# The reverse scan of a preparation queued behind the decays' scan of the one before

## The chip, the cores and the metric

The kernel runs on one core of a Trainium2 chip. The core has a matrix engine (TensorE, PE in the profile), a vector engine (VectorE, DVE), a scalar engine (ScalarE, ACT), GpSimd (POOL) and SyncE (SP), which here only starts transfers; 16 DMA engines move data between HBM and the on-chip memory. Each engine works through its own queue of instructions in the order in which they were put there, and waits at an instruction until what it needs is there. The metric is device time in microseconds for the whole program.

## The reference

Two parts follow each other: a linear-attention recurrence over 768 steps for 4 batches of 8 heads with head dimension 40, and a soft mixture of 8 expert networks over the 3072 resulting tokens.

```python
for t in range(S):                       # state: (B, H, 40, 40), S = 768
    y[:, :, t] = einsum('bhd,bhde->bhe', r[t], state)
    Sa = einsum('bhde,bhe->bhd', state, a[t])
    state = state * w[t][:, :, None, :] - einsum('bhd,bhe->bhde', Sa, b[t])
    state = state + einsum('bhd,bhe->bhde', v[t], k[t])
x = y.transpose(0, 2, 1, 3).reshape(3072, 320)
P = exp(x @ w_gate - max)                # 8 rounds of row and column normalisation follow
out = sum over e of P[:, e] * (relu(x @ w1[e]) @ w2[e])    # 320 -> 1024 -> 320
```

All is float32. The decay `w` lies near 0.9 for every step and every column of the state.

## The kernel before

**Attention in chunks.** The 768 steps are cut into 12 chunks of 64, so that a chunk of one batch becomes a few small matrix products. A *preparation* `prep(c, b)` does what depends only on the inputs of chunk c and batch b; there are 48, numbered `cb = 4c + b` from 0. It loads one input block (`inp`, L120: decays, k, b and a), and then:

- the *reverse scan* `q` (L126, VectorE): running products of the decays from the end of the chunk backwards, 112 rows of 260. There is one buffer `q` for all preparations;
- the reciprocal `g1` of the whole chunk's decay (L130, VectorE; one buffer);
- the *decays' scan* `ge` (L135, VectorE): running products from the front, started with `g1`. It is written into the preparation's *set* (tiles `sx`, `bb`, `cc`, `ge`; some sets lie in one raw tile named `st` in the profile). There are 19 sets used in turn (`NSX`), so preparation n writes where n-19 was;
- `kb` = k and b times q (L146) and `cc`, a copy out of q (L151), both on GpSimd (the first `kb` on VectorE); `ab` = a times the decays (L152, L153, on GpSimd from the seventh preparation on), four small matmuls `ll` (L158) and four transposes `kt` (L166) on TensorE, the masked copy `sx` (L168, VectorE), copies on ScalarE (L154, L155, L172 to L175), and the part `lt` sent to HBM (`ld`, L177).

The input block of most preparations has two buffers; the load of the one after next waits for the `ab` product that reads a buffer last.

**The inversion.** Two chunks (8 preparations) form a group. Their triangular matrices are read back from HBM (`load_lu`, L370) and inverted on VectorE: `flip_l` (two copies, L199 and L200, the inversion's first), multiply and reduce pairs (L183/L186, L192/L195) into `un` and `tn`, with a last copy at L360. There are six groups and so six inversions. The inverses go to HBM and come back (`tload`, L239 to L246), and TensorE completes them (`gp` L255, `op` L261) to the matrix `tt` of a chunk.

**The recurrence.** `recur(c, b)` has per chunk and batch: loads `rv` (L269) and `f` (L271), matmuls `av` (L280) and a masked copy `f` (L281, VectorE), `xc` (L288) and copies `x` and `c` (L294, L295), `pu` (L299) with the masked copy `pm` (L301, VectorE), `c2` (named `c`, L306) with the sum `ws` (L308, VectorE), the output `y` = ws times the set's decays (L312, GpSimd; it is the last reader of the set's `ge`), and the next state `z` (L321) with its transposes (L326).

**Expert layers.** From about 460 us on TensorE runs them nearly without a break (L571 first layer, L636 second).

**What sets the order.** The program text lists the pieces of preparation, inversion and recurrence in the order of due times:

```python
t = max(t, t0 + P0[s] + PD * i) if s else -20 + 0.01 * i
ev.append((t, do_prep, (s,) + cb + (i == 0,)))
...
for _, fn, args in sorted(ev, key=lambda x: x[0]):
    fn(*args)
```

That order is only a priority. A planner of the framework then walks through the program on a simulated clock, and whenever an engine comes free it gives it, of the instructions that are ready by that clock, the one that is earliest in the text. The result is fixed at build time as one queue for each engine. From the ninth block of the expert layers on (`N_MAN`) the order of the text is kept on all engines but SyncE. `tc.issue_after(ins)` adds to each instruction in its block that goes to the engine of `ins` an ordering edge behind `ins`, without a semaphore.

Of the kernel before, what the change touches and what calls it, by code (L numbers as in the profile page):

```python
# [3 lines left out]

# [10 lines left out]
ALU = mybir.AluOpType  # L15
# [14 lines left out]
def attention(ctx, tc, d, xd, ps, pq, pt, gs, lg):  # L30
    nc = tc.nc
# [13 lines left out]
    one65 = cst[0:RL, 400:660]  # L45
# [55 lines left out]
    def first_use(i):  # L101
        if i in fresh:
            fresh.discard(i)
            nc.gpsimd.memset(bb_b[i], 0.0)
            nc.scalar.copy(out=sx_b[i][64:R2].rearrange("r p h x -> r (p h) x")[:, :, 64:104],
                           in_=cst[64:R2, 360:400].unsqueeze(1).broadcast_to([40, 8, 40]))
# [3 lines left out]
    def rot(key, lst):  # L110
        i = state[key]
        state[key] = (i + 1) % len(lst)
        return lst[i]

    zp = [None] * NB

    def prep(c, b, ld):
        cb = c * NB + b
        inp = raws[IN_MAP[cb]][0:RL, 0:1032] if IN_MAP.get(cb) else pin.tile([RL, 1032], F32, name="inp", bufs=2)
        nc.sync.dma_start(out=inp, in_=d["inp"][c, b, :, 0:1032])  # L120
        w65 = inp[:, 0:264]
        kb_in = inp[0:R2, 264:776].rearrange("r (p k t) -> r p k t", p=NP, k=2)
        a_in = inp[:, 776:1032].rearrange("r (p t) -> r p t", p=NP)
        qr = pin.tile([RL, NP, 65], F32, name="q")
        q = qr[:, ::-1]
        nc.vector.tensor_tensor_scan(  # L126
            out=qr.rearrange("r p t -> r (p t)"), data0=w65[:, 260:0:-1], data1=one65,
            initial=0.0, op0=ALU.mult, op1=ALU.add)
        g1 = rot("g1", g1_b)
        nc.vector.reciprocal(out=g1[:, :, 0], in_=q[:, :, 64])  # L130
        sx = rot("sx", sx_b)
        i = next(j for j in range(NSX) if sx_b[j] is sx)
        bb, cc, ge = bb_b[i], cc_b[i], ge_b[i]
        g = ge[:, :, 0:64]
        nc.vector.tensor_tensor_scan(  # L135
            out=ge.rearrange("r p t -> r (p t)"), data0=w65[:, 0:260],
            data1=g1.rearrange("r p t -> r (p t)"), initial=0.0, op0=ALU.mult, op1=ALU.add)
        if cb < NKB:
            raw = raws[KB_SETS[cb % len(KB_SETS)]]
            kb = raw[0:R2, 0:512].rearrange("r (p k t) -> r p k t", p=NP, k=2)  # L140
            lt = raw[0:64, 512:1024].rearrange("r (p k t) -> r p k t", p=NP, k=2)
        else:
            kb = pin.tile([R2, NP, 2, 64], F32, name="kb")
            lt = pin.tile([64, NP, 2, 64], F32, name="lt")
        eng = nc.vector if cb < NFAST else nc.gpsimd
        (nc.gpsimd if cb in KB_POOL else eng).tensor_tensor(  # L146
            out=kb, in0=kb_in,
            in1=q[0:R2, :, 63::-1].unsqueeze(2).broadcast_to([R2, NP, 2, 64]), op=ALU.mult)
        ab = rot("ab", ab_b)
        first_use(i)  # L150
        nc.gpsimd.tensor_copy(out=cc, in_=q[0:R2, :, 64])  # L151
        eng.tensor_tensor(out=ab[0:40, :, 0:64], in0=a_in[0:40], in1=g[0:40], op=ALU.mult)  # L152
        eng.tensor_tensor(out=ab[64:104, :, 64:128], in0=a_in[64:104], in1=g[64:104], op=ALU.mult)  # L153
        nc.scalar.copy(out=sx[64:104, :, 0, 0:64], in_=ab[0:40, :, 0:64])  # L154
        nc.scalar.copy(out=sx[64:104, :, 1, 0:64], in_=ab[64:104, :, 64:128])  # L155
        ll = pq.tile([128, NP, 2, 64], F32, name="ll", tag="pq")
        for p in range(NP):
            nc.tensor.matmul(ll[:, p], lhsT=kb[:, p], rhs=ab[:, p], start=True, stop=True)  # L158
        if cb < NKB:
            nc.scalar.activation(out=lt, in_=ll[64:128], func=AF.Copy, scale=-1.0)  # L160
            (nc.sync if cb < N_SP else nc.scalar).dma_start(out=ld[GRP[c][1], :, b], in_=lt)
            kt = pt.tile([128, NP, 2, 64], F32, name="kt", tag="pt")
        else:
            kt = pq.tile([128, NP, 2, 64], F32, name="kt", tag="pq")
        for p in range(NP):
            nc.tensor.transpose(kt[:, p].rearrange("s h x -> s (h x)")[:, 0:R2],  # L166
                                kb[:, p].rearrange("r k s -> r (k s)"), ident[0:R2, 0:R2])
        nc.vector.tensor_tensor(  # L168
            out=sx[0:64, :, :, 0:64], in0=ll[0:64],
            in1=mask_u.unsqueeze(1).unsqueeze(1).broadcast_to([64, NP, 2, 64]), op=ALU.mult)  # L170
        if cb >= NKB:
            nc.scalar.activation(out=lt, in_=ll[64:128], func=AF.Copy, scale=-1.0)  # L172
        nc.scalar.copy(out=sx[0:64, :, :, 64:104], in_=kt[0:64, :, :, 0:40])
        nc.scalar.activation(out=bb[0:64, :, 0:40], in_=kt[64:128, :, 0, 0:40], func=AF.Copy, scale=-1.0)
        nc.scalar.activation(out=bb[64:128, :, 64:104], in_=kt[64:128, :, 1, 0:40], func=AF.Copy, scale=-1.0)  # L175
        if cb >= NKB:
            (nc.sync if cb < N_SP else nc.scalar).dma_start(out=ld[GRP[c][1], :, b], in_=lt)  # L177
        return dict(cc=cc, g=g, sx=sx, bb=bb)
# [201 lines left out]
    def do_prep(s, c, b, first):  # L380
        if first:
            start_seg(s)
        preps[c, b] = prep(c, b, invs[s][0])

    for c in range(NCH):
# [3 lines left out]
        t = 5 * c + 2 - T_LEAD  # L389
        ev.append((t - L_LEAD, tload, (c,)))  # L390
        ev.append((t, tmat, (c,)))
    for s, cs in enumerate(GROUPS):
# [3 lines left out]
        for i in range(n):  # L396
            cb = (cs[0] + i // NB, i % NB)
            j = cb[0] * NB + cb[1] - NSX
            t = 5 * (j // 4) + 3 + SKEW * (j % 4) + 0.01
            t = max(t, t0 + P0[s] + PD * i) if s else -20 + 0.01 * i  # L400
# [27 lines left out]
N_SP = 8  # L428
# [25 lines left out]
def body(ctx, tc, d, out):  # L454
# [9 lines left out]
    with ExitStack() as actx:  # L464
        ps, pq, pt = (actx.enter_context(tc.tile_pool(name=f"a_ps{i}", bufs=n, space=bass.MemoryType.PSUM))
                      for i, n in enumerate((PC, PQ, PT)))
        nc.sync.dma_start(out=gs, in_=d["gate"])
        attention(actx, tc, d, xd, ps, pq, pt, gs, lg)
# [356 lines left out]
```

## Time and profile before

| what | value |
|---|---|
| median of 3 runs (lowest to highest) | 1821.08 us (1817.26 to 1829.43) |
| the profiled execution's own time | 1816.42 us |
| its span | 1814.0 us |
| busy PE, DVE, ACT, POOL | 1686.0, 1366.1, 842.8, 876.6 us |
| q scans (L126) from tile `inp`: count, busy, idle of VectorE before them | 42, 34.1 us, 36.4 us |

A row of the groups gives line, engine, operation, output and inputs by their names, shapes and count; then busy time and the mean of one in ns; then the idle time of the engine just ahead of them and what ended it. A row of the timeline gives start and duration in us, the engine, the line and the instruction, and in brackets how long the engine stood idle before it and what ended that. The slices of the page give busy tenths of forty equal parts of the span.

### The profile page before, as it was taken

The page shows a single profiled execution, that of the slowest core. Times are in us where ns is not written, and L with a number is a line of the kernel's source. Part 1 is how long each engine was busy: PE and PEld are TensorE (multiplying, and loading weights), DVE is VectorE, ACT ScalarE, POOL GpSimd, SP SyncE. Part 2 cuts the span into 40 slices and gives each one's busy share as a digit, 9 for nine tenths or more (in the row PEclk, how much of TensorE's full clock was granted, in tenths as well). Part 3 has the DMA queues.
Part 4 walks back from the last instruction along what each step waited for, and adds up shares of the span by engine and source line. Part 5 has one row for each costly group of instructions (what it writes and reads, how often), then busy time and mean ns, then how long its engine had stood idle before and what let it go on. Part 6 is the DMA issues. An engine that isn't in the chain of part 4 may idle for free.

```text
span 1814.0 us, 32745 instructions
## 1 busy us (share of the span) xinstructions
PE 1686.0 (93%) x12611; PEld 1662.1 (92%) x12611; DVE 1366.1 (75%) x2353; ACT 842.8 (46%) x1811; POOL 876.6 (48%) x850
## 2 busy tenths in 40 slices
PE   5478888987889999999999999999999999999999
PEld 4367888887889999999999999999999999999999
DVE  7886976974788777767686778867686777768675
ACT  6357767765634443424343443435343443434342
POOL 7555645724453554728173554009173553719160
PEclk7569989998989999999999999999999999999999
DMA  7478678668221111102010112202010111102001
GB/s 200 106 160 197 150 173 192 153 142 200 75 67 36 41 38 38 58 20 76 8 69 20 57 38 72 58 1 76 14 63 22 55 38 38 58 20 76 18 21 44
DMA packets 178736, 135.61 MB, mean 75 GB/s; under 512 B 119189, under 2 KB 160789, under 8 KB 178581
## 3 DMA queue, kind: packets, MB, share of 16 engines
q1 hardware_dynamic: 174901, 127.79, 26.8%
q10 hardware_dynamic: 3680, 5.74, 1.2%
q8 instruction: 99, 1.62, 0.4%
q14 instruction: 56, 0.46, 0.1%
HBM read 111.48 MB, written 22.02 MB: 74 GB/s over the span
## 4 chain that ended last, share of the span: by engine, by line
PE 72%; DVE 6%; DMA 2%; issue 1%; SPq 1%; ACT 1%; POOL 1%; DVEq 0%; ACTq 0%; POOLq 0%
PE op L636 37%; PE p L571 34%; DVE pr L192 1%; DVE sm L589 1%; DVE hl L595 1%; DVE gt L195 0%; DMA ld<-lt 0%; PE xc L288 0%; DMA rv<-in_rv_dram 0%; DVE un L195 0%; PE pu L299 0%; DVE u L589 0%; DMA ws<-in_wts_dram 0%; DVE xch L559 0%; DMA lu<-ld 0%
## 5 line engine op out<-in xcount | busy, mean ns | idle before, releaser
L571 PE MATMUL p<-xch,wh 128*128 128x384 f32 (+1 forms) x1792 | 605.7, 339 | 10.2 <-DVE u L589 4.3
L592 ACT ACTIVATE hh<-sm 128x384 fp32r<-128x384 f32 x512 | 269.4, 527 | 723.0 <-DVE sm L589 722.9
L636 PE MATMUL op<-wh,hh 128*128 128x320 f32 x1536 | 477.1, 311 | 1.1 <-ACT hh L592 0.9
L636 PE MATMUL op<-wl,hh 128*128 128x320 f32 x1536 | 474.8, 310 | 0.0
L636 PE MATMUL op<-wh,hl 128*128 128x320 f32 x1536 | 468.2, 310 | 0.9 <-DVE hl L595 0.9
L517 POOL TENSOR_TENSOR wl<-ws,wh 128x640 fp32r<-128x640 f32 x60 | 103.6, 1726 | 606.3 <-ACT wh L515 606.1
L595 DVE SCALAR_TENSOR_TENSOR hl<-sm,hh 128x384 fp32r<-128x384 f32 x512 | 375.0, 766 | 1.8 <-ACT hh L592 1.3
L571 PEld LDWEIGHTS p<-xch,wh 128*128 128x128 f32 (+1 forms) x1792 | 337.2, 188 | 14.3 <-DVE u L589 6.0
L571 PE MATMUL p<-xcl,wh 128*128 128x384 f32 x896 | 302.6, 338 | 0.0
L571 PE MATMUL p<-xch,wl 128*128 128x384 f32 x896 | 301.7, 337 | 0.0
L636 PEld LDWEIGHTS op<-wh,hh 128*128 128x128 f32 x1536 | 290.3, 189 | 2.2 <-ACT hh L592 1.9
L636 PEld LDWEIGHTS op<-wl,hh 128*128 128x128 f32 x1536 | 291.1, 190 | 0.0
L636 PEld LDWEIGHTS op<-wh,hl 128*128 128x128 f32 x1536 | 287.3, 188 | 1.3 <-DVE hl L595 1.2
L589 DVE TENSOR_TENSOR sm<-p,u 128x384 f32<-128x384 f32 x384 | 236.1, 625 | 8.8
L571 PEld LDWEIGHTS p<-xcl,wh 128*128 128x128 f32 x896 | 168.7, 188 | 0.0
L571 PEld LDWEIGHTS p<-xch,wl 128*128 128x128 f32 x896 | 168.6, 188 | 0.0
L589 DVE TENSOR_TENSOR sm<-p,p 128x384 f32<-128x384 f32 x128 | 71.3, 557 | 128.7 <-PE p L571 74.7
L589 DVE TENSOR_TENSOR p<-p,p 128x384 f32<-128x384 f32 x128 | 71.2, 556 | 99.6 <-PE p L571 99.1
L589 DVE TENSOR_TENSOR u<-p,p 128x384 f32<-128x384 f32 x128 | 70.8, 554 | 57.6 <-PE p L571 56.4
L158 PE MATMUL ll<-ab,kb 104*128 104x128 f32 x336 | 62.4, 343 | 51.8 <-POOL ab L153 32.3
L158 PEld LDWEIGHTS ll<-ab,kb 104*128 104x128 f32 x336 | 53.4, 241 | 58.3 <-POOL ab L153 35.8
L525 POOL TENSOR_TENSOR wl<-ss,wh 128x512 fp32r<-128x512 f32 x60 | 90.1, 1502 | 27.6 <-ACT wh L522 23.4
(164 smaller groups left out, 2637.0 us busy)
## 6 DMA issues: line engine op xcount, KB each, us to landing
ws<-in_wts_dram SPq DMA_DIRECT2D x60, 832.0 KB, 4.4
inp<-in_inp_dram SPq DMA_DIRECT2D x42, 451.5 KB, 4.8
rv<-in_rv_dram SPq DMA_DIRECT2D x48, 336.0 KB, 4.1
xd<-y SPq DMA_DIRECT2D x24, 224.0 KB, 3.1
ld<-lt ACTq DMA_DIRECT2D x40, 128.0 KB, 2.9
f<-in_vt_dram SPq DMA_DIRECT2D x48, 80.0 KB, 3.1
out_dram<-acc SPq DMA_DIRECT2D x42, 80.0 KB, 2.1
lu<-ld SPq DMA_DIRECT2D x24, 128.0 KB, 3.2
```

The lines of the kernel that those rows point to most:

```text
L158: nc.tensor.matmul(ll[:, p], lhsT=kb[:, p], rhs=ab[:, p], start=True, stop=True)
L192: nc.vector.tensor_tensor(out=prv, in0=a.unsqueeze(2).broadcast_to([nu, n_c, n_r, n_k]), in1=m.unsqueeze(1).broadcast_to([nu, n_c, n_r, n_ ...
L517: g.tensor_tensor(out=wl[:, 0:640], in0=raw[:, 256:896], in1=wh[:, 0:640], op=ALU.subtract)
L525: g.tensor_tensor(out=lv[:, 3:7], in0=so[:, :, 0], in1=hv[:, 3:7, 0], op=ALU.subtract)
L571: nc.tensor.matmul(o, lhsT=w_, rhs=x_, start=(j == 0), stop=(j == 3))
L589: eng.tensor_tensor(out=out, in0=x, in1=y, op=ALU.add)
L592: nc.scalar.activation(out=hh[:, f, h], in_=sm[f][:, h], func=AF.Relu)
L595: v.scalar_tensor_tensor(out=hl[:, f, h], in0=sm[f][:, h], scalar=0.0, in1=hh[:, f, h], op0=ALU.max, op1=ALU.subtract)
L636: nc.tensor.matmul(ops[i], lhsT=a[:, h, cs], rhs=w_[:, cw], start=(f == 0 and h == 0 and j == 0), stop=(last and h == 1 and j == 2))
```

## The change

The scan `ge` of every preparation is noted in a list as it is written. From preparation 8 on (`N_SP` is 8, so the ninth) the reverse scan `q` is written inside a block that orders it on VectorE behind the last noted `ge`, which is that of the preparation before. The first eight preparations are untouched. No operation, buffer or transfer is added or taken away.

```diff
+    scans = []
 
     def prep(c, b, ld):
...
         qr = pin.tile([RL, NP, 65], F32, name="q")
         q = qr[:, ::-1]
-        nc.vector.tensor_tensor_scan(
-            out=qr.rearrange("r p t -> r (p t)"), data0=w65[:, 260:0:-1], data1=one65,
-            initial=0.0, op0=ALU.mult, op1=ALU.add)
+        with tc.issue_after(scans[-1].ins) if cb >= N_SP else nullcontext():
+            nc.vector.tensor_tensor_scan(
+                out=qr.rearrange("r p t -> r (p t)"), data0=w65[:, 260:0:-1], data1=one65,
+                initial=0.0, op0=ALU.mult, op1=ALU.add)
         g1 = rot("g1", g1_b)
         nc.vector.reciprocal(out=g1[:, :, 0], in_=q[:, :, 64])
...
-        nc.vector.tensor_tensor_scan(
+        scans.append(nc.vector.tensor_tensor_scan(
             out=ge.rearrange("r p t -> r (p t)"), data0=w65[:, 0:260],
-            data1=g1.rearrange("r p t -> r (p t)"), initial=0.0, op0=ALU.mult, op1=ALU.add)
+            data1=g1.rearrange("r p t -> r (p t)"), initial=0.0, op0=ALU.mult, op1=ALU.add))
```

More of the change, by code (lines that the diff above doesn't have):

```diff
@@ L1 @@
 from collections import deque
-from contextlib import ExitStack
+from contextlib import ExitStack, nullcontext
 from functools import partial
```

## The prediction

> **What bounds the kernel now.** I began with the page: the span, then the busy tenths.
>
> ```profile
> span 1814.0 us, 32745 instructions
> ...
> PE   5478888987889999999999999999999999999999
> ...
> DVE  7886976974788777767686778867686777768675
> ...
> DMA  7478678668221111102010112202010111102001
> ```
>
> The profiled execution took 1816.42 us, 2.42 more than its span, and lies 4.66 under the median of 1821.08. From the thirteenth slice on (each is 45.35 us) PE stands at 9 throughout and DMA at 2 and below: the expert layers run on TensorE, their first matmuls at 459 us. The preparations lie ahead of that, their last scan at 359:
>
> ```profile
> 459.11 0.60 PE L571 MATMUL p<-xch,wh 128*128 128x384 f32 x2
> ```
> ```profile
> L135 DVE TENSOR_TENSOR_SCAN st<-inp,g x17: 681/700/1674, 46.6 to 359.0; 112x260 f32<-112x260 f32 x17
> ```
>
> So the change can move the time only by letting the attention part end sooner or later. The windows show what is full there.
>
> ```profile
> 272.00:317.00 45.00, 37.41 (x444) 35.97 (x445) 28.68 (x54) 32.19 (x81) 25.29 (x33) 0.93 0.89 193
> 317.00:363.00 46.00, 41.63 (x494) 40.15 (x493) 45.55 (x79) 35.97 (x91) 34.53 (x35) 0.96 0.63 154
> ```
>
> The columns are the stretch, its length, busy PE, PEld, DVE, ACT and POOL, granted clock, DMA share, GB/s. In the first stretch the DMA engines are 89% busy and VectorE 64%; in the second VectorE is busy 45.55 of 46 us. VectorE is an in-order queue here, and the groups by form say what it stands for in front of a q scan:
>
> ```profile
> L126 DVE TENSOR_TENSOR_SCAN q<-inp,cst 112x260 f32<-112x260 f32 x42 | 34.1, 811 | 36.4 <-DMA inp<-in_inp_dram 30.3 <-POOL kb L146 6.0
> ```
>
> 30.3 us it waited for the load of a preparation's input, with everything queued behind the scan waiting too.
>
> **What the change touches.** I matched the n-th q scan with the n-th decays' scan (48 each) in VectorE's timeline. Counting preparations from 0, q(n+1) stands ahead of the decays' scan ge(n) at ten places, n = 19, 22, 25, 26, 27, 35, 37, 41, 43, 44; from preparation 8 on it stands behind it everywhere else already. So 30 of the 40 new orderings hold in the queue of before, and ten pairs swap. Nothing is added or removed: no scan, no DMA. Both ends of the new edge are on VectorE, where order needs no wait. No instruction moves past another queue by the edge itself.
>
> Why q overtook: there are 19 sets, so ge(n) writes into the set whose decays the y product of preparation n-19 (GpSimd) reads last. ge(n) is ready at the end of that y; q(n+1) needs only its input and the free q buffer. The first of the ten and the last:
>
> ```profile
> 123.35 2.18 POOL L312 TENSOR_TENSOR y<-ws,ge 104x256 f32<-104x256 f32 x1
> ```
> ```profile
> 126.02 0.88 DVE L135 TENSOR_TENSOR_SCAN ge<-inp,g 112x260 f32<-112x260 f32 x1
> ```
> ```profile
> 337.00 0.69 POOL L312 TENSOR_TENSOR y<-ws,ge 104x256 f32<-104x256 f32 x1
> ```
> ```profile
> 339.24 0.67 DVE L135 TENSOR_TENSOR_SCAN ge<-inp,g 112x260 f32<-112x260 f32 x1
> ```
>
> The scans come 0.49 and 1.55 us after their y ended (125.53, 337.69). Over the ten places this lateness sums to 17.9 us, the largest 5.11 (n=41) and 3.20 (n=25): that is all that the swap itself can give. I go through the places with the rest of each queue held as it is.
>
> **n=41.**
>
> ```profile
> 307.40 0.57 DVE L308 TENSOR_TENSOR ws<-c,c 104x416 f32<-104x416 f32 x1
> 312.74 0.70 DVE L126 TENSOR_TENSOR_SCAN q<-inp,cst 112x260 f32<-112x260 f32 x1 [4.77 <-DMA inp<-in_inp_dram]
> 313.36 0.56 DVE L301 TENSOR_TENSOR pm<-pu,cst 128x416 f32<-128x416 f32 x1
> 313.84 0.69 DVE L135 TENSOR_TENSOR_SCAN ge<-inp,g 112x260 f32<-112x260 f32 x1
> ...
> 315.74 0.49 DVE L199 COPY lu<-lu 128x128 f32<-128x128 f32 x1 [0.94 <-DMA lu<-ld]
> ```
> ```profile
> 307.00 1.06 PE L299 MATMUL pu<-x,tt 128*128 128x104 f32 x8
> ```
> ```profile
> 308.05 0.68 POOL L312 TENSOR_TENSOR y<-ws,ge 104x256 f32<-104x256 f32 x1 [0.42 <-DVE ws L308]
> ```
>
> q(42) waits 4.77 us for its input, and behind it stand the recurrence's pm (its pu was there at 308.06) and ge(41) (its y ended at 308.73). Swapped, pm runs at 308.1, ge(41) at 308.7, q(42) still at 312.74. That looks like 5 us, but the next thing in the queue is the first copy of the fifth inversion, which waits for its matrix until 315.74 either way, and the recurrence's next f and ws stand behind that copy. I take it at 0. If the planner also put that f ahead of the copy, the full stretch after it would be shorter by it, and with pm and ge (0.56, 0.69) that is some 1.9 us:
>
> ```profile
> L281 DVE TENSOR_TENSOR f<-av,cst 104x512 f32<-104x512 f32 x48 | 32.5, 678 | 14.6 <-PE av L280 13.8 <-DMA nd<-tn 0.5
> ```
>
> **n=25.**
>
> ```profile
> 171.07 0.70 DVE L126 TENSOR_TENSOR_SCAN q<-inp,cst 112x260 f32<-112x260 f32 x1 [2.84 <-DMA inp<-in_inp_dram]
> 171.69 0.67 DVE L135 TENSOR_TENSOR_SCAN ge<-inp,g 112x260 f32<-112x260 f32 x1
> ...
> 175.69 0.27 DVE L199 COPY lu<-lu 128x128 f32<-128x128 f32 x1 [2.47 <-DMA lu<-ld]
> ```
> ```profile
> 167.81 0.68 POOL L312 TENSOR_TENSOR y<-ws,ge 104x256 f32<-104x256 f32 x1
> ```
> ```profile
> 173.98 2.08 PE L158 MATMUL ll<-ab,kb 104*128 104x128 f32 x8 [3.67 <-POOL ab L153]
> ```
>
> ge(25) was ready at 168.49 and VectorE was free; it ran at 171.69, and PE stood 3.67 us at the preparation's matmuls. Swapped, those come 3.2 us sooner; but here too the next copy of an inversion waits for its load until 175.69, and what the recurrence has next on VectorE is queued behind it. Taken at 0; 3.2 if that cover is gone.
>
> **n=26 and n=37**, where the DMA wait of q is short and VectorE has other work:
>
> ```profile
> 179.55 0.56 DVE L183 TENSOR_TENSOR pr<-un,lu 128x64 f32<-128x64 f32 x1
> 180.61 0.70 DVE L126 TENSOR_TENSOR_SCAN q<-inp,cst 112x260 f32<-112x260 f32 x1 [0.50 <-DMA inp<-in_inp_dram]
> 181.23 0.68 DVE L135 TENSOR_TENSOR_SCAN ge<-inp,g 112x260 f32<-112x260 f32 x1
> ```
> ```profile
> 277.91 0.67 DVE L168 TENSOR_TENSOR sx<-ll,cst 64x512 f32<-64x512 f32 x1
> 279.39 0.83 DVE L126 TENSOR_TENSOR_SCAN q<-inp,cst 112x260 f32<-112x260 f32 x1 [0.81 <-DMA inp<-in_inp_dram]
> 280.14 1.19 DVE L195 TENSOR_REDUCE un<-pr 128x64 f32<-128x1024 f32 x1
> 281.25 0.68 DVE L135 TENSOR_TENSOR_SCAN ge<-inp,g 112x260 f32<-112x260 f32 x1
> ```
> ```profile
> 278.99 0.67 POOL L312 TENSOR_TENSOR y<-ws,ge 104x256 f32<-104x256 f32 x1
> ```
>
> n=26: ge at 180.11, q at 180.79, both done at 181.49 in place of 181.91: 0.42. n=37: the reduce at 278.58, ge at 279.77 (its y ended at 279.66), q at 280.45, done at 281.28 in place of 281.93: 0.65. Both lie in queues that are nearly full, so I count them on the path. The other six (n = 19, 22, 27, 35, 43, 44) trade one scan for the other in a queue that goes on at once or meets the same y: 0 each, bounded by their lateness of 6.3 together above, and below by one scan of 0.7 at each for q(n+1), which its readers on GpSimd would feel, 4.2 together. That cover is the y of the next preparation: the scan after next cannot start before it, some 7 us later.
>
> Sum: 0.42 + 0.65 = 1.1 us sooner; 1815.3 for the profiled execution, 1820.0 from the median.
>
> One thing speaks against it: with ge(n) first, the ab products that wait for ge on GpSimd run while q(n+1) is on VectorE. Such a pair stands in the trace already:
>
> ```profile
> 321.81 1.19 DVE L126 TENSOR_TENSOR_SCAN q<-inp,cst 112x260 f32<-112x260 f32 x1
> ```
> ```profile
> 321.58 0.86 POOL L152 TENSOR_TENSOR ab<-inp,ge 40x256 f32<-40x256 f32 x1
> ```
>
> q took 1.19 there in place of 0.70. At ten places that is 4.9 us at most; I take 0, since at six of the ten q waits for its load anyway (below). The Trainium skill, page "SBUF — State Buffer", section "Who interferes with whom", has the rule: a VectorE instruction with two SBUF inputs and a GpSimd one that reads SBUF shut each other out for a whole instruction. The 1.19 agrees; by the rule the sum would be 4.9 - 1.1 = 3.8 us slower, 1825.
>
> **Rivals.** (a) All the lateness is on the path: ge(n) sets ab, ll and the buffer of the next input. For it: PE's 3.67 us above. Against: the two copies that wait for their loads anyway. 17.9 us give 1803; with the six waits of q for its input at the swapped places gone as well (1.55 and 0.39 below, 2.84, 0.50, 0.81 and 4.77 above, 10.9 in all), 1792.
>
> ```profile
> 147.67 0.70 DVE L126 TENSOR_TENSOR_SCAN q<-inp,cst 112x260 f32<-112x260 f32 x1 [1.55 <-DMA inp<-in_inp_dram]
> ...
> 189.14 0.92 DVE L126 TENSOR_TENSOR_SCAN q<-inp,cst 112x260 f32<-112x260 f32 x1 [0.39 <-DMA inp<-in_inp_dram]
> ```
>
> (b) Loads set the pace: where DMA is 89% busy an earlier ge only brings an earlier request into a full queue. Then nothing moves: 1821.
>
> (c) Slower. The planner lays out every queue anew, SyncE's too. The input's load waits there for the ab that frees its buffer:
>
> ```profile
> SPq L120 <- POOL ab L153: 13.1, 9, 2.7
> ```
>
> That is between 100 and 320 us: 13.1 us in 9 waits, the longest 2.7. If the new plan, which thinks ge(n) earlier, puts that load ahead of the recurrence's rv and f loads, SyncE stands at it, and these land late. Ten such places at 2.7 are 27: 1821 - 1 + 27 = 1847. It decides against the change by over 1% from the eighth of them on ((18.2 + 1.1) / 2.7).
>
> (d) It does not do what it says: the planner keeps the ten q scans where they were in time and holds ge too, or the swap is undone by other work put between. 1821.
>
> **How the numbers follow.** Forecast 0.45, a 0.18, b 0.15, c 0.15, d 0.07. The time is the forecast's, 1820. Its own range is 1815 (1.9 and 3.2 from the covers gone) to 1825 (4.2 from q's readers and half a microsecond over). About what a measurement of this kernel can tell from no change is 1%, 18 us: under 1803, over 1839. Faster takes most of (a), 0.14; slower most of (c), 0.12; 0.74 are left for the middle. The range reaches half-way into (a) and (c): 1802 to 1837.
>
> **What would show it.** VectorE's timeline has ge(n) ahead of q(n+1) at all ten places, and its lateness after the y falls to some 0.7 us; the 30.3 us that q waits for its input stay within a few us; the inversions' first copies start at the same times to 2 us; the first expert matmul (459 us) moves by no more than 3. A first expert matmul that moves by over 10 us would prove the forecast wrong, and the inversion whose first copy moved first would say by which rival.

## The result, and the profile after

Over 14 runs each the median went from 1821.68 to 1812.07 us: 9.6 us between the medians. The ratio of the runs, by which all kernels are compared here, is 0.9942 with a 95% interval from 0.9925 to 0.9959. That is 10.6 us faster (7.5 to 13.7). The forecast was 1820.0 in a range from 1802 to 1837; it said that the time would stay within 1%, which it does, but it gave the change 1.1 us.

The profiled execution of the changed kernel took 1813.25 us, that of before 1816.42. The latter was a quick draw, 5.3 us under its median, so the two traces show less of a difference than the runs. In the changed kernel the lines of a preparation ahead of the scan q have moved down by one, those from the scan on by two. The page after:

```profile
span 1811.3 us, 32736 instructions
...
PE   5468978898889999999999999999999999999999
...
DVE  6887986974788677768686778867686777767675
...
DMA  8478688577311111102010112202010111102001
```

It is the same picture: TensorE at 9 from the thirteenth slice on. The difference lies ahead of that. The recurrence's last y on GpSimd, in the timeline of before and then of the changed kernel (start, duration, in brackets the idle time before it and what ended it):

```profile
488.22 1.40 POOL L312 TENSOR_TENSOR y<-ws,st 104x256 f32<-104x256 f32 x1 [2.77 <-DVE ws L308]
```
```profile
483.31 0.94 POOL L314 TENSOR_TENSOR y<-ws,st 104x256 f32<-104x256 f32 x1 [4.41 <-DVE ws L310]
```

The attention part ends 5.4 us sooner (489.62 and 484.25). From there to the end of the profiled execution it is 1326.8 us before and 1329.0 after, 2 us more; the last section has what ends in these 2 us. The first expert matmul, in the timeline of the changed kernel, has moved the other way, from 459.11 to 460.71:

```profile
460.71 0.60 PE L573 MATMUL p<-xch,wh 128*128 128x384 f32 x2
```

The two windows of the prediction, of the changed kernel (stretch, length, busy PE, PEld, DVE, ACT, POOL, granted clock, DMA share, GB/s):

```profile
272.00:317.00 45.00, 38.18 (x460) 36.74 (x459) 29.48 (x55) 32.66 (x83) 26.82 (x33) 0.92 0.89 199
317.00:363.00 46.00, 40.63 (x479) 39.11 (x479) 42.78 (x73) 34.32 (x86) 29.75 (x34) 0.93 0.56 139
```

DMA is as full in the first as it was (0.89). VectorE is busy for 42.78 us of the second, where it was 45.55. The place n=41 in VectorE's timeline, and the group of the q scans:

```profile
303.12 0.93 DVE L137 TENSOR_TENSOR_SCAN ge<-inp,g 112x260 f32<-112x260 f32 x1 [0.20 <-POOL y L314]
...
307.24 0.70 DVE L128 TENSOR_TENSOR_SCAN q<-inp,cst 112x260 f32<-112x260 f32 x1 [3.19 <-DMA inp<-in_inp_dram]
307.86 0.56 DVE L303 TENSOR_TENSOR pm<-pu,cst 128x416 f32<-128x416 f32 x1
...
312.96 0.29 DVE L201 COPY lu<-lu 128x128 f32<-128x128 f32 x1 [3.87 <-DMA lu<-ld]
```
```profile
L128 DVE TENSOR_TENSOR_SCAN q<-inp,cst 112x260 f32<-112x260 f32 x42 | 33.1, 789 | 23.8 <-DMA inp<-in_inp_dram 19.0 <-POOL kb L148 4.7
```

ge(41) now runs the moment its y ends (0.03 us behind it, 5.11 before), ahead of q(42). Over the ten places the lateness is 7.9 us, 0.79 each; it was 17.9. The loads that q waits for cost VectorE 19.0 us of idle time instead of 30.3.

The planner, though, did more than swap ten pairs. Compared position by position, 341 of VectorE's 2353 queue places hold another instruction than before, 984 of TensorE's 10586, 355 of ScalarE's, 92 of GpSimd's and 144 of SyncE's.

### The profile page after: what moved, and what is told of

It is laid out like the page before. It is cut to its first block, busy times and chain, and to the rows that moved or that the text cites. A ratio compares the mean times of both kernels' runs of the same rounds, so it can differ in the third digit from the quotient of the medians.

```text
span 1811.3 us, 32736 instructions
## 1 busy us (share of the span) xinstructions
PE 1691.7 (93%) x12611; PEld 1668.9 (92%) x12611; DVE 1361.3 (75%) x2353; ACT 842.0 (46%) x1811; POOL 868.8 (48%) x850
## 4 chain that ended last, share of the span: by engine, by line
PE 75%; DVE 11%; DMA 5%; issue 3%; POOL 2%; SPq 2%; ACT 2%; ACTq 0%; DVEq 0%; POOLq 0%
PE op L638 36%; PE p L573 34%; DVE pr L194 1%; PE xc L290 1%; DVE q L128 1%; DMA lu<-ld 1%; PE pu L301 1%; SPq L248 1%; DMA inp<-in_inp_dram 1%; DVE un L197 1%; DMA rv<-in_rv_dram 1%; DVE sm L591 1%; DVE gt L197 1%; POOL ab L154 1%; DMA ld<-lt 1%
## 5 line engine op out<-in xcount | busy, mean ns | idle before, releaser
L597 DVE SCALAR_TENSOR_TENSOR hl<-sm,hh 128x384 fp32r<-128x384 f32 x512 | 368.5, 753 | 1.9 <-ACT hh L594 1.3
```

What stands on the lines that cost most here:

```text
L597: v.scalar_tensor_tensor(out=hl[:, f, h], in0=sm[f][:, h], scalar=0.0, in1=hh[:, f, h], op0=ALU.max, op1=ALU.subtract)
```

## The experiments

Two theories stood against each other. By the first, the swap of the ten pairs is the cause: ge is no longer held up, and what comes sooner reaches the end. By the second, the new edge only nudges the planner into another layout of all the queues, and the time lies there. Times below are ratios to the kernel before, run beside it, with 95% intervals; microseconds are the ratio on 1821.

**The swap alone, twice.** All five queues of before are written out by hand in the program, as a chain of ordering edges that lets the planner choose nothing. Only the ten q scans move. In the diff, n stands for 19, 22, 25, 26, 27, 35, 37, 41, 43, 44.

```diff
+def queue_up(nc, tc):
+    for numbers in QUEUES.values():       # those of the kernel before
+        for x, y in zip(numbers, numbers[1:]):
+            tc.add_manual_dep(by[f"I-{y}"], f"I-{x}", info, reason="queue_up")
...
 # VectorE's queue, at ten n
-    q(n+1)
     ...
     ge(n)
+    q(n+1)
```

> Every engine's queue of the kernel before is written out by hand, and on VectorE alone the ten q scans are put right behind the decays' scan that they overtook; nothing else moves. Theory A (the gain comes from the planner's new layout of all queues, not from the swap): the last y product in the profile comes 0 to 2 us sooner than before's 489.6, and the time is 0 to 3 us under before's. Theory B (the swap itself gives it, by the lateness of the decays' scans): the last y near 483, the time 7 to 11 us under before's.

> All ten pairs swapped in the queues of before, again, against the same runs of before as the two runs above. The first time it was 7.7 us under before's (4.9 to 10.4). If the swap is about three quarters of the change's gain: 6 to 9 us under before. If that first value was high by chance: 3 to 5.

Measured: 0.9958 (0.9943 to 0.9973), and in the repetition 0.9974 (0.9959 to 0.9989). Together 0.9966, some 6.2 us. The first value is the one that the lateness theory named, and the repetition's 4.7 us lie where its expectation put them if the first was high by chance. So the swap does reach the end without any help of the planner, with more than five times the 1.1 us that the forecast gave it. The q scans' group in the first of the two:

```profile
L128 DVE TENSOR_TENSOR_SCAN q<-inp,cst 112x260 f32<-112x260 f32 x42 | 33.4, 794 | 28.2 <-DMA inp<-in_inp_dram 22.8 <-POOL kb L148 5.3
```

With nothing but the swap, the load waits fall from 30.3 to 22.8 us. Of this fall 6.7 us lie at the six swapped places where q had waited for its load: ge now runs inside the wait, at n=41 pm too, and less of it is left. The scans q themselves came hardly sooner: q(23), q(26) and q(42) started 1.01, 2.57 and 4.01 us behind the end of the y of their place before, and 0.89, 2.29 and 3.58 us with the swap.

**The changed kernel again**, for the planner's share.

> The changed kernel again, on the same chip and against the same runs of before as the three kernels above: 8 to 12 us under before's. If the ten swaps alone explain it, it lies within 3 us of them.

Measured: 0.9944 (0.9926 to 0.9962). With the first measurement that is 0.9943, some 10.4 us. Over the swap alone it is 4.2 us, plus or minus 3; the expectation had set 3 us as the most that the ten swaps alone would leave.

**Half of the edges each, planner free.**

```diff
-with tc.issue_after(scans[-1].ins) if cb >= N_SP else nullcontext():
+with tc.issue_after(scans[-1].ins) if N_SP <= cb < 32 else nullcontext():   # the first half
+with tc.issue_after(scans[-1].ins) if cb >= 32 else nullcontext():          # the second half
```

> The ordering edge for preparations 8 to 31 alone. The plan is the changed kernel's up to there. Theory A: the third inversion ends 3 to 5 us sooner than before (231.4), as in the changed kernel (227.5), and the recurrence's seventeenth product (before 264.9, changed 259.5) comes 4 to 6 us sooner; how much of it is left at the last y depends on the plan behind it, and I expect 3 us, so a time 3 to 5 us under before's. Theory B: five of the ten swaps, lateness 8.5 of 17.9 us, so half the gain, 4 to 5 us, without a shorter third inversion.

> The ordering edge for preparations 32 to 47 alone; the plan is before's up to there. Theory A: the third inversion as before (231.4), what is gained comes from the new layout between 265 and 490 us: last y 2 to 5 us sooner, time 2 to 5 us under before's. Theory B: the other half of the lateness, 9.4 us, half the gain.

Measured: the first half 0.9971 (0.9957 to 0.9985), 5.3 us; the second half 0.9991 (0.9978 to 1.0004), 1.6 us, which can't be told from nothing. By these medians the larger part belongs to the edges up to preparation 31, though the intervals overlap. The first half came out about as the layout theory had it, with the shorter stretch about the third inversion that is shown further on; the second half by its median missed both theories, and in its profile the last y ended at 494.8 us, later than before.

**One edge, at q(42).** This is the place with the longest lateness, n=41, and here the planner changed but three places of VectorE's queue and three of GpSimd's.

```diff
-with tc.issue_after(scans[-1].ins) if cb >= N_SP else nullcontext():
+with tc.issue_after(scans[-1].ins) if cb == 42 else nullcontext():
```

> The edge for preparation 42 alone; the queues are before's but for three places each on VectorE and GpSimd: pm and the decays' scan of 41 now stand ahead of q(42), which waited 4.77 us for its load. By the prediction's step the inversion's first copy still waits for its matrix until about 315.7 and nothing is gained behind it: last y within 2 us of 489.6. The rival: the recurrence's next products come 3 to 5 us sooner and stay so.

A single run, 1822.10 us. VectorE's timeline at the place, and GpSimd's two y products about it:

```profile
310.88 0.59 DVE L303 TENSOR_TENSOR pm<-pu,cst 128x416 f32<-128x416 f32 x1 [0.20 <-PE pu L301]
311.48 0.93 DVE L137 TENSOR_TENSOR_SCAN ge<-inp,g 112x260 f32<-112x260 f32 x1
...
316.13 0.70 DVE L128 TENSOR_TENSOR_SCAN q<-inp,cst 112x260 f32<-112x260 f32 x1 [3.72 <-DMA inp<-in_inp_dram]
...
319.00 0.27 DVE L201 COPY lu<-lu 128x128 f32<-128x128 f32 x1 [1.90 <-DMA lu<-ld]
```
```profile
310.76 0.68 POOL L314 TENSOR_TENSOR y<-ws,ge 104x256 f32<-104x256 f32 x1 [0.40 <-DVE ws L310]
...
321.52 0.68 POOL L314 TENSOR_TENSOR y<-ws,ge 104x256 f32<-104x256 f32 x1 [4.37 <-DVE ws L310]
```

Here pm and ge(41) ran at once, 5 us sooner against their y than before, exactly as the prediction described the swap. The next y still came 10.8 us after this one (10.5 before): the inversion's copy waits for its matrix, and the recurrence stands behind it. The term of 0 for n=41 held at this place. The last y of this run ended at 495.7 us, 6 us later than before, and not within the 2 us that were expected; the granted clock from the first to the last y was 0.89, where before's was 0.92, so the single run can't test the end.

**The ten places in groups**, all with the queues of before held and the q scans of the named n alone moved:

```diff
 # VectorE's queue: places swapped
-    none
+    22, 25, 26, 27, 37, 41          # q waits for its load
+    19, 35, 43, 44                  # the rest of the ten
+    25, 26, 27                      # another cut
+    19, 22, 35, 37, 41, 43, 44      # what that leaves
+    22, 37, 41
```

> The queues of before with six of the ten pairs swapped: those whose q scan waited for its load (n = 22, 25, 26, 27, 37, 41). Theory C (the gain of the swap is the load's wait, which before stood in front of the decays' scan and all that needs it): nearly all of the gain of swapping ten, 5 to 8 us under before. Theory D (any scan put one place earlier gains, about equally): six tenths of it, 3 to 5 us.

> The queues of before with the other four pairs swapped (n = 19, 35, 43, 44), where q did not wait for a load. Theory C: 0 us, within 1.5 either way. Theory D: 2 to 4 us under before.

> The queues of before with three neighbouring pairs swapped (n = 25, 26, 27; lateness 6.4 of 17.9 us). The prediction's steps for them are 0, 0.42 and 0: 0.4 us under before. Theory E (a scan that is late at one place delays the y that the next one waits for, so that neighbouring places add up and the loads behind them move too): 2 to 4 us under before.

> The queues of before with the other seven pairs swapped (n = 19, 22, 35, 37, 41, 43, 44; lateness 11.5 us). The prediction's step: 0.65 us under before, from n = 37. Theory E: 4 to 5 us under before, and with the three of the other run about the sum of ten swaps.

> The queues of before with three pairs swapped at n = 22, 37 and 41, the places whose q waited 1.55, 0.81 and 4.77 us for its load and that are not neighbours (lateness 8.3 us). The prediction's steps: 0, 0.65 and 0, so 0.7 us under before. Theory C (the wait in front of the decays' scan is what the swap takes off the path, here above all the 4.77 at n = 41): 2.5 to 5 us under before. If the time is within 1.5 us of before's, the swap's gain cannot be put to single places with these runs.

| places swapped | ratio (95%) | us | the forecast's terms |
|---|---|---|---|
| 22, 25, 26, 27, 37, 41 | 0.9968 (0.9952 to 0.9985) | -5.8 | -1.1 |
| 19, 35, 43, 44 | 0.9985 (0.9969 to 1.0001) | -2.7 | 0 |
| 25, 26, 27 | 0.9998 (0.9982 to 1.0015) | -0.4 | -0.4 |
| 19, 22, 35, 37, 41, 43, 44 | 0.9983 (0.9968 to 0.9999) | -3.1 | -0.65 |
| 22, 37, 41 | 0.9982 (0.9968 to 0.9997) | -3.3 | -0.65 |

The first two rows are one cut of the ten, the next two another; they add up to -8.5 and -3.5, on either side of the -6.2 of all ten, and each interval is some 3 us to either side. The medians of all groups but 25 to 27 lie above the forecast's terms, but only the first row excludes its term (2.7 to 8.7 us faster, for 1.1); the interval of 22, 37 and 41 (0.5 to 5.8) still holds its 0.65. None of the theories in the expectations is decided by these rows. By the medians the load's wait as the whole cause (C) fits the first row and not the 2.7 of the second, equal gains at each place (D) the second and not the first, and neighbours that add up (E) would have given 2 to 4 us for 25 to 27. Of n=37 there is a row to look at. VectorE with the swap (22, 37, 41) and without it (19, 35, 43, 44), and the y products about it on GpSimd, each pair in that order:

```profile
283.28 0.93 DVE L137 TENSOR_TENSOR_SCAN ge<-inp,g 112x260 f32<-112x260 f32 x1
284.14 0.67 DVE L128 TENSOR_TENSOR_SCAN q<-inp,cst 112x260 f32<-112x260 f32 x1
```
```profile
281.15 0.73 DVE L128 TENSOR_TENSOR_SCAN q<-inp,cst 112x260 f32<-112x260 f32 x1 [0.91 <-DMA inp<-in_inp_dram]
...
282.92 0.68 DVE L137 TENSOR_TENSOR_SCAN ge<-inp,g 112x260 f32<-112x260 f32 x1
```
```profile
282.57 0.68 POOL L314 TENSOR_TENSOR y<-ws,ge 104x256 f32<-104x256 f32 x1
287.64 0.68 POOL L314 TENSOR_TENSOR y<-ws,ge 104x256 f32<-104x256 f32 x1
```
```profile
280.65 0.68 POOL L314 TENSOR_TENSOR y<-ws,ge 104x256 f32<-104x256 f32 x1
286.43 0.68 POOL L314 TENSOR_TENSOR y<-ws,ge 104x256 f32<-104x256 f32 x1
```

From the start of one y to that of the next it is 5.07 us with the swap and 5.78 without. Over eight profiles (that of before, and those of the held queues with nothing but swaps) the mean with the swap lies 0.72 us under the mean without, where the forecast had 0.65. Read in the same way, n=22 and 41 give 0.3 each, 26 and 27 give 0.2 each, and the others lie between a loss of 0.4 and a gain of 0.1. All places together come to 0.8 us. The 6.2 us that the runs show are not found in the local readings.

**q gives way to everything that is ready.** To the ten swaps come four q scans, n+1 = 25, 34, 40 and 41, moved further behind the recurrence's or an inversion's next instructions, so that less stands behind their loads.

```diff
 # VectorE's queue, with the ten swaps
-    q(25), its reciprocal; ws, pm
+    ws, pm; q(25), its reciprocal
-    q(40), its reciprocal; four of the inversion
+    four of the inversion; q(40), its reciprocal
 # and alike q(34) behind ws, pm; q(41) behind f; on GpSimd two y, z ahead of cc, kb
```

> All ten pairs swapped, and four further q scans that still wait 17 us in all for their loads (25, 34, 40, 41) moved behind the next instructions of VectorE that do not need them (the recurrence's ws and pm, the inversion's next three pairs, f); on GpSimd two y products with their z are moved ahead of the copy and the product out of q. Theory C: the wait for the load is filled with the recurrence's work, the last y comes 2 to 6 us sooner than with ten swaps alone, and the time is 3 to 7 us under it, 10 to 14 under before's. The rival: those waits lay beside another wait (the y that the decays' scan needs, the matrix of the next inversion), and the time stays within 2 us of the ten swaps'.

The group of the q scans in it:

```profile
L128 DVE TENSOR_TENSOR_SCAN q<-inp,cst 112x260 f32<-112x260 f32 x42 | 33.8, 805 | 14.9 <-DMA inp<-in_inp_dram 9.2 <-POOL kb L148 5.4
```

Measured: 0.9965 (0.9948 to 0.9982), 6.4 us, the same as the ten swaps alone. The load waits fell from 22.8 to 9.2 us, and 13.6 us of them were worth nothing that can be told (0.2 us, plus or minus 4). That is what the rival of the expectation had said: they lay beside other waits. Which ones is not shown place by place.

**What the planner's layout gives.** This is read from traces; no run took it alone. The stretch from the tenth to the sixteenth y, in which the third inversion ends, in windows of before, of the swap alone, of the kernel with the seven swaps, and of the changed kernel:

```profile
196.30:239.10 42.80, 37.56 (x339) 35.90 (x338) 36.74 (x56) 32.28 (x81) 31.54 (x36) 0.96 0.65 167
```
```profile
194.20:237.00 42.80, 37.58 (x340) 35.93 (x339) 36.62 (x56) 32.31 (x80) 31.31 (x36) 0.96 0.64 164
```
```profile
197.10:237.90 40.80, 36.04 (x338) 34.17 (x337) 37.15 (x56) 32.29 (x80) 31.06 (x36) 1.00 0.69 173
```
```profile
197.80:235.70 37.90, 34.63 (x366) 33.11 (x367) 34.98 (x54) 31.59 (x79) 29.35 (x37) 1.00 0.76 181
```

In the eleven profiles whose early queues are before's, or nearly so, the stretch takes 40.8 to 41.4 us at a granted clock of 1.00 (three profiles), 42.7 to 42.8 at 0.96 (four) and 43.4 to 44.4 at 0.92 (four). The changed kernel has 37.9 and 38.5 in its two profiles, and the first half of the edges 38.5, all three at 1.00. At an equal clock the new layout is thus some 2.7 us shorter here (41.0 and 38.3 on the mean), and in its three profiles the clock did not fall, as it did in eight of the eleven. What makes the clock fall can be seen in windows of 3.41 us of the same stretch, of before, laid so that they begin and end where the granted clock steps:

```profile
204.66:208.07 3.41, 2.90 (x27) 2.53 (x26) 3.41 (x5) 2.81 (x7) 2.71 (x4) 1.00 0.41 84
208.07:211.48 3.41, 1.77 (x17) 1.60 (x16) 3.41 (x6) 1.20 (x4) 3.12 (x5) 1.00 0.76 142
211.48:214.89 3.41, 3.41 (x22) 3.41 (x21) 3.41 (x5) 2.81 (x8) 2.81 (x1) 0.50 0.98 221
214.89:218.30 3.41, 3.41 (x36) 3.41 (x35) 3.25 (x7) 2.79 (x7) 1.79 (x3) 1.00 0.52 113
...
221.72:225.13 3.41, 2.22 (x23) 2.04 (x21) 3.41 (x5) 2.73 (x8) 3.33 (x3) 1.00 0.48 129
225.13:228.54 3.41, 2.45 (x24) 2.45 (x25) 2.21 (x5) 1.27 (x4) 3.00 (x5) 1.00 0.50 137
```

TensorE is busy for 1.77 us of the second window; in the one behind it the clock is 0.50, and then 1.00 again. Half of 3.41 us is 1.7 us, about the step from 41.0 to 42.8. The hollow comes at a matmul of a preparation that waits 1.64 us for its ab; the same timeline of the changed kernel has the recurrence's matmuls in its place, and none of its windows there, laid on its own steps, has TensorE busy for less than 2.5 us. The Trainium skill, page "TensorE: Matmul & The Clock Gate", section "What's actually happening", says that the array's clock drops to half after an idle window of about 3.4 us, and that these windows run free of the program. The length and the half agree with the rows; that it takes a window without work does not, since TensorE did 1.77 us of work in this one.

How much work it takes can be counted. In the fourteen profiles kept of all these kernels, from 120 to 460 us and in windows laid in this way, 86 windows at full clock had TensorE busy for under 1.7 us, and 85 of them were followed by one at half clock. Of the 956 with 2.1 us or more 16 were. So a hollow counts by how it falls on the windows: the second one here leaves TensorE busy for 1.25 us from 223.50 to 226.90, but a window ends in its midst, the two windows have 2.22 and 2.45 us of work, and the clock stays at 1.00.

## Why the prediction was right or wrong

**The time.** The measured time lies in the range, and the way it moved is the forecast's, but the range is 35 us wide. By the sum the change was worth 1.1 us, and it is worth 10.6. That the time came out inside is the width of the range, not the mechanism. (Half-way from the forecast's own range, 1815 to 1825, to the rivals' 1792 and 1847 would be 1803.5 and 1836, not 1802 and 1837; nothing hangs on that.)

**Right.** The swap is made at all ten places, and the lateness fell to 0.79 us, where some 0.7 was named. The 0.65 of n=37 measured 0.72 from y to y. The 0.42 of n=26, with nothing for 25 and 27, measured 0.4 for the three, but the interval (from 3.3 us faster to 2.7 slower) is too wide to test such a term, and the agreement is luck. At n=41 nothing came of 5 us, for the reason given. The first expert matmul moved by 1.6 us, under 3; but it was no sign of the end, since the experts' first matmuls run among the last of the recurrence, whose own end came 5.4 us sooner.

**Wrong, first step: "with the rest of each queue held as it is".** The places were gone through on that premise, and it doesn't hold: the planner lays out all queues anew, from about VectorE's 175th place on. The swap without that is worth 6.2 us, the changed kernel 10.4. The rival that took the planner up, (c), gave it the wrong sign by way of SyncE; SyncE's waits ahead of the input's loads between 100 and 320 us came to 30.6 us before and 29.7 after. That the layout is better where the third inversion ends is read, not tested by itself.

**Wrong, second step: the sum of 1.1 us.** It measures 6.2 with all else held. The smallest group that can be told from zero is 22, 37 and 41: 3.3 us (0.5 to 5.8) for 0.65; in the local readings the three have 1.3. The four places 19, 35, 43 and 44 measured 2.7 us for 0, in an interval that touches zero. The terms that the prediction set to 0 because another wait covers them are thus small at their own places, and yet the sum is 5 us too small. Where these 5 us lie is open.

The granted clock, which the sum leaves out, points to a part of them. It is on record for every run: 0.9511 on the mean of the 100 runs of before beside the experiments, 0.9536 over the 18 of the swap alone. As time lost to it (the span times what the clock is short of 1) that is 89.0 and 84.2 us, 4.9 us less, plus or minus 1.7. Among the 100 runs of before one that lost 1 us more took 0.63 us longer, so by that estimate some 3 of the 6.2 us go with the clock. It is no proof: no run holds the clock fixed, shorter waits of TensorE may be what raised it, and the kernel with 22, 37 and 41 was 3.3 us faster at 0.9503. The clock is also a reason not to look for these us in single profiles: with the same queues but for a few swaps the attention part from first to last y took 357.1 to 366.7 us at a clock of 0.91 to 0.92, and 368.5 to 369.8 at 0.88 to 0.90.

**Wrong: "the 30.3 us that q waits for its input stay within a few us".** They fell to 19.0, and to 22.8 with the swap alone. Most of the fall with the swap alone follows from the prediction's own steps: where ge, and at n=41 pm, run ahead of a q whose load lands as before, the wait is shorter by what now runs in it, and this was not carried over to the sign. It cost little: in the kernel in which q gives way 13.6 us less of these waits gave nothing that can be told.

**Wrong: the inversions' first copies within 2 us.** The first three came within 2 us (54.2, 105.8 and 175.2 us, against 52.5, 104.1 and 175.7), the last three 3 us sooner (237.5, 313.0 and 373.7, against 240.7, 315.7 and 376.4). The fourth is the first to move, so the third inversion's stretch, which the prediction counted at nothing, is where the lead was made; 1.7 us of it are the window of half clock that before's profile has there.

**Rivals.** (a) gave 17.9 us for lateness that is all on the path. The swap alone took the lateness to 3.0 us in each of its two profiles and is worth 6.2 us, so most of it is not. (b) and (d) are out, since the time moved and the swap was made. The rule on shared access, by which the sum would have been 3.8 us slower, doesn't show: a q scan took 789 and 809 ns on the mean in the two profiles of the changed kernel, and 811 before, and all 96 scans together 80.0 and 81.8 us, and 81.3 before.

## What to carry to other kernels

An ordering edge given to a planner is two changes: the order itself, and a new layout of everything that the planner decides after it. Write the old queues out by hand with the one move to tell them apart, and when forecasting give the layout a range of its own (here some 4 us of 10). An instruction that waits at the head of an in-order queue is worth moving behind what is ready, but the idle time put down to it is no measure of the gain: 30.3 us of it could be cut to 22.8 with 6 us of gain and on to 9.2 with no more that could be told.

## What the runs showed that was not expected

The same queues give different times in one stretch, in steps: 41.0, 42.8 and about 43.8 us at a granted clock of 1.00, 0.96 and 0.92, as none, one or two windows of half clock follow the hollows of TensorE in it. The first such step is 1.7 us, more than either term of the forecast's sum, so a single profile can't show terms of that size in the sum of a stretch. Where a hollow falls on the clock's windows differs from execution to execution (the clock's first step came at 19.6 to 23.2 us of the fourteen profiles), so part of each measured time is chance that no queue decides.

The 2 us that the changed kernel's profile takes longer behind the last y are such a step. From there to the end it took 1326.8 us before, and 1329.0 and 1329.9 in the two profiles of the changed kernel; both of these have one window of half clock among the expert layers' matmuls (it begins at 589.8 and 585.5 us), and before's has none behind 512 us until the end. Over all fourteen profiles the seven with such a window (it begins between 585 and 602 us) took 1327.9 to 1329.9 us, four of them with queues of before and a few swaps, and the seven without it 1326.4 to 1327.1. So what is given back there is mostly the clock, and no cost of the change is shown.
